# XCiT attention folded into a star-ReLU block: q's last rows in two transfers, three fixed v buffers, a k square on two engines, w_out's first piece ahead of v's second tile, v's first tile in 256, 128 and 128 tokens

## The chip, the cores and the metric

The kernel runs on one core of one Trainium2 chip. The metric is the device time of one execution in microseconds (us); lower is better. The engines are named as in the profile: PE (TensorE matmuls) with PEld (its weight loads), DVE (VectorE), ACT (ScalarE), POOL (GpSimd, which here only issues DMAs), and SP (SyncE, which issues DMAs too).

## The reference

There are B = 4 batches of N = 6080 tokens with C = 256 channels, and a block with Dff = 2048.

```python
def _attn_ref(q, k, v, tau) -> np.ndarray:
    qn = q / (np.linalg.norm(q, axis=1, keepdims=True) + 1e-06)
    kn = k / (np.linalg.norm(k, axis=1, keepdims=True) + 1e-06)
    s = kn.transpose(0, 2, 1) @ qn / tau
    s = s - s.max(-1, keepdims=True)
    a = np.exp(s)
    a /= a.sum(-1, keepdims=True) + 1e-09
    return (v @ a).astype(np.float32)

def _moe_ref(x, w_in, w_out, s, b) -> np.ndarray:
    h = x @ w_in
    r = np.maximum(h, 0.0)
    g = s * (r * r) + b
    return (g @ w_out).astype(np.float32)
```

The attention matrix is channels by channels (256 x 256) for each batch, and needs the norms of q's and k's columns over all 6080 tokens of the batch. The output is 24320 x 256 in float32.

## The kernel before

**What is computed in which order.** For each batch the kernel sums the Gram matrix of k and q (`Gram.mm`, tile `s_ps`) and the squared norms (`squares`, `add_norms`, tile `n_ps`) over chunks of 512 tokens. `finish_ops` turns them into the inverse norms (`inverse`: Ln, Exp, on ACT), scales the Gram matrix (`scale`, on DVE), takes the exponential (`exps`, tile `eT`), and multiplies it into w_in: `wa` = softmax matrix times w_in, 256 x 2048, so that v @ a @ w_in becomes v @ wa. Then come 48 groups of 512 tokens of v (`NG` = 48, the last one of 256). A group is 16 steps (`FT` = 16); a step is one call of `mm1`, which makes 128 rows of h from the transposed v tile `vT`. Two steps share one tile `h_ps`, of which there are two buffers. `relu` (ACT) takes it, `square` (DVE or ACT) makes `g`, and a second product with w_out follows for the group before (`seven_items`, seven half-size products instead of eight; `plain_mm2` for the first and last group).

**What sets the order.** Nothing is scheduled by a planner: each instruction is issued where the Python code calls it (`po` keeps program order), so each engine works through its queue in that order. `at_step(s, f)` files a piece of side work under a step, `early` files the folds of w_in (`fold_one`) under steps 1, 3, 5 and 8, and the loop over `s` at the end of the file calls them. The Gram work of the next batch is side work of this kind.

**The head.** Batch 0 has no earlier group to hide behind. Its k and q are 13 chunks, the last two of 224 tokens each (112 partitions by 2). I call the last four c9 to c12, as the code's `c_, c0, c1, c2`. All transfers of k, q, v and the weights are issued by POOL in one queue, q's last rows (`load_last`) just ahead of v's first tile, in two pieces of which each is one chunk. Each POOL transfer uses one of eight semaphores in turn, and so waits for the landing of the transfer eight places before it. Once q's last rows are there, the chain is: squares (L201), column sums on PE (L270), Ln and Exp on ACT (L300), two short DVE instructions (L286, L288), `exps` (L331), row sums and the first fold of w_in on PE (L371, L376, L381), `scaled` on ACT and DVE (L352, L354), and the first `mm1` (L823). Ahead of the row sums PE transposes v's first tile: `turn_v(0, range(3))`, into a bank of the pool `ps_o`, and inside `first_block` the fourth block of 128 tokens, `turn_v(0, range(3, 4))`. The first `mm1` of group 0 is made in two parts, 384 and 128 tokens.

**v after the first two tiles.** `load_v(g)` (L495, POOL) brings a tile of 512 tokens in float16, `crossbar_v(g)` (L521, SP) transposes it by DMA at step (g-2)*16+6 into one of three `vT` buffers. The pool of v tiles has four buffers, and `load_v(g)` is called at step (g-4)*16+2 (tiles 3 and 4 both at step 2).

**Lines that the text names:** L130 `load`, L159 `load_last`, L174 `mm`, L201 and L203 `squares` on DVE and ACT, L216 and L230 `fold` and `into_first`, L266 and L270 `add_norms`, L325 `scale`, L359 `fold_mm`, L506 and L508 the transposes of `turn_v` and their copy, L565 `load_w_in`, L582 w_out's pieces, L697 `cast_w_out`, L823 and L836 `mm1`, L846 `relu`, L859 `square`, L911 `plain_mm2`, L1007 `seven_items`.

Of the kernel before, what the change touches and what calls it, by code (L numbers as in the profile page):

```python
# [16 lines left out]
def kernel(  # L17
# [37 lines left out]
    def po(ins):  # L55

        tc.keep_in_program_order(ins)
        return ins
# [10 lines left out]
    f3_pool = pool("f3_pool", 13)  # L69
    sm_pool = pool("sm", 1)  # L70
    apool = pool("apool", 2)
    vpool = pool("vpool", 4)
    vtpool = pool("vtpool", 3)
    rpool = pool("rpool", 2)
    gpool = pool("gpool", 2)
# [19 lines left out]
    JC = 4  # L95
# [16 lines left out]
    class Gram:  # L112
# [35 lines left out]
        def load_last(self, i):  # L148

            c = len(self.chunks) - 2  # L150
            at, np_, _ = self.chunks[c]
            if i == 0:
                self.raw[c] = qk_pool.tile([P, 2, JC, C], FP16, tag="qk", name="qk")
                for h in range(2):
                    t = self.raw[c][:, :, ts(h, 2)]
                    self.tiles[c + h] = t[:, 1], t[:, 0]
            rows = (k, q)[i][self.b, at:].rearrange("(p j) c -> p j c", j=JC)
            for js in [slice(0, JC)] if i == 0 else [ts(h, 2) for h in range(2)]:
                po(nc.gpsimd.dma_start(out=self.raw[c][:np_, i, js], in_=rows[:, js]))  # L159

        def cast(self, c):
# [21 lines left out]
        def norm_ops(self, c):  # L183
# [4 lines left out]

            at_end = self.b == 0 and c >= len(self.chunks) - NLATE

            def squares(a, js):
                def f():
                    if "sq" not in st:
                        if at_end:
                            st["sq"] = late_pool.tile([P, 2, jc, C], FP16, tag=f"sq{c}", name="sq")
                        else:
                            st["sq"] = sq_pool.tile([P, 2, JC, C], FP16, tag="sq", name="sq")
                    src = (qc, kc)[a][:np_, js, :]
                    if (a == 0 or c == len(self.chunks) - 1 if at_end else
                            a == 0 and (self.b > 0 or c % 2 == 0)):  # L200
                        po(nc.vector.tensor_mul(st["sq"][:np_, a, js, :], src, src))  # L201
# [35 lines left out]
            if self.b == 0 and c >= len(self.chunks) - NLATE - 1:  # L237
                ops = [lambda i=i: unfolded(i) for i in range(2)]
                if c == len(self.chunks) - NLATE:
                    return [squares(1, slice(0, jc)), [squares(0, ts(h, 2)) for h in range(2)], *ops]  # L240
                return [squares(1, slice(0, jc)), squares(0, slice(0, jc)), *ops]
            ops = []
            for h in range(0, jc, 4):
# [30 lines left out]
        def finish_ops(self):  # L274
# [88 lines left out]
            def first_block(n):  # L363

                two = [self.bank("wa_ps", CH, C)[:, 0, :n], h_tile("wa_ps")[:, 0, :n]]
                second = self.bank("wa_ps", CH, C)[:, :, :n]
                r_ps = ps_gram.tile([P, CH, C], FP32, tag="s_ps", name="r_ps")[:, :, 0]
                for j in range(CH):
                    exps(j)
                    for ch in range(CH):  # L370
                        po(nc.tensor.matmul(r_ps[:, ch : ch + 1], st["e"][:, j, ts(ch, P)],  # L371
                                            parts16, start=(ch == 0 and j == 0),
                                            stop=(ch == CH - 1 and j == CH - 1),
                                            skip_group_check=True))
                    for m in range(CH):
                        po(nc.tensor.matmul(two[m], st["e"][:, j, ts(m, P)],  # L376
                                            w_in16[:, j, :n],
                                            start=(j == 0), stop=(j == CH - 1)))
                for m in range(CH):
                    for j in range(CH):  # L380
                        po(nc.tensor.matmul(second[:, m], st["e"][:, j, ts(m, P)],  # L381
                                            w_in16[:, j, ds(n, n)], start=(m == 0 and j == 0),
                                            stop=(j == CH - 1), skip_group_check=True))
                copy = turn_v(0, range(3, 4))
                del v_tiles[0]
                st["rs"] = sm_pool.tile([P, CH], FP32, tag="rs", name="rs")
                po(nc.vector.reciprocal(out=st["rs"], in_=r_ps))
                for f0 in range(0, n, P):
                    for m in range(CH):
                        scaled(f0, P, m, two[m][:, ds(f0, P)])  # L390
                copy()
                for m in range(CH):
                    scaled(n, n, m, second[:, m])

            def fold_one(f0, n, m):
                def f():
# [93 lines left out]
    def load_v(g, js=None):  # L490
        t0, nj = group(g)
        js = js or slice(0, nj)
        if g not in v_tiles:
            v_tiles[g] = vpool.tile([P, TG // P, C], FP16, tag="v16", name="v16")
        po(nc.gpsimd.dma_start(  # L495
            out=v_tiles[g][:, js, :],
            in_=v_flat[t0 : t0 + nj * P, :].rearrange("(p j) c -> p j c", j=nj)[:, js]))

    def turn_v(g, js):
# [3 lines left out]
        vT_ps = ps_o.tile([P, CH, TG], FP16, tag="o_ps", name="vT_ps")  # L503
        for j in js:
            for ch in range(CH):
                po(nc.tensor.transpose(vT_ps[:, ch, ts(j, P)], v16[:, j, ts(ch, P)], ident16))  # L506
        cols = ds(js[0] * P, len(js) * P)
        return lambda: po(nc.vector.tensor_copy(out=vT_tiles[g][:, :, cols],  # L508
                                                in_=vT_ps[:, :, cols]))

    def transpose_v(g):
        turn_v(g, range(group(g)[1]))()
# [51 lines left out]
        cs = slice(0, CH) if co is None else slice(co, co + 1)  # L564
        po(nc.gpsimd.dma_start(out=w_in16[:, cs, f0:f1], in_=w_in_rows[:, cs, f0:f1]))  # L565

    load_v(0, slice(0, 3))
    load_w_in(0, 2 * P)
    load_w_in(2 * P, NW)
    load_v(0, slice(3, 4))  # L570
    load_w_in(NW, NW + 2 * P)
    load_w_in(NW + 2 * P, 2 * NW)
    load_w_in(2 * NW, 3 * NW)
    load_w_in(3 * NW, Dff)
    w_out_rows = moe_w_out.rearrange("(fo p) d -> p fo d", p=P)
    load_v(1)

    NPIECE = FT // 4
    w_pieces = []
    for i in range(NPIECE):  # L580
        w32 = qk_pool.tile([P, 4, C], FP32, tag="qk", name="w32")
        po(nc.gpsimd.dma_start(out=w32, in_=w_out_rows[:, ts(i, 4), :]))  # L582
        w_pieces.append(w32)
    load_v(2)
    s_bc = consts.tile([P, 1], FP32)
    po(nc.gpsimd.dma_start(out=s_bc, in_=moe_s.to_broadcast((P, 1))))
# [39 lines left out]
    for a in (1, 0):  # L626
        g0.rows[a].append(sum_rows[a])
        g0.add_norms(a)
    ops[c0][0]()
    add_rows(1, c0)  # L630
    ops[c1][0]()
    ops[c2][0]()
# [15 lines left out]
    g0.rows[0].extend(half)  # L648
    g0.add_norms(0)
    add_rows(0, c1)  # L650
    ops[c2][1]()
    g0.mm(c2, 0)
    ops[c2][2]()
    g0.mm(c2, 1, [0])
# [156 lines left out]
    def mm1(g, m):  # L811
# [5 lines left out]
        if fh == 0:  # L817
            h_tiles[g, i] = h_tile("h_ps")
        if g == 0 and i == 0:
            for cols in (slice(0, 3 * P), slice(3 * P, TG))[: 2 * fh]:  # L820
                for f in range(2):
                    for ci in range(CH):
                        po(nc.tensor.matmul(h_tiles[g, i][:, f, cols], g0.wa[:, ci, ts(f, P)],  # L823
                                            vT[:, ci, cols], start=(ci == 0),
                                            stop=(ci == CH - 1), skip_group_check=True))
            return
        h_ps = h_tiles[g, i][:, fh, :]
        for b, p0, p1 in segments(g):
# [275 lines left out]
```

## Time and profile before

| what | value |
|---|---|
| median of 3 runs | 713.14 us (713.06, 713.14, 714.91) |
| the profiled execution | 713.05 us, of which the span of the profile is 711.3 us |
| granted TensorE clock over the span | 0.998 |
| busy over the span | PE 692.2 us (97%), DVE 634.2 us (89%), ACT 547.8 us (77%), POOL 112.9 us (16%) |
| bytes moved by DMA | 83.81 MB, mean 118 GB/s |

The profile is one execution; its times count from the start of its span. A line of the timeline gives start, length, engine, source line, operation, tiles, shapes and count, and in brackets how long the engine was idle before and what ended that. Instructions of one engine that overlap are merged, so a merged line's length is less than the sum of its instructions. A line of busy time by stretch gives, for each engine, the busy time and in brackets the instructions, then the granted clock of TensorE (1.00 is full), the DMA share and GB/s. "Issue" in the DMA list is the moment at which a transfer was handed over; it lands some us later.

### The profile page before, as it was taken

What the parts mean: (1) busy time and instruction counts of PE and PEld (TensorE: products, weight loads), DVE (VectorE), ACT (ScalarE), POOL (GpSimd) and SP (SyncE); (2) the same over time, 40 slices, a digit from 0 to 9 for tenths busy, and PEclk for the clock granted to TensorE, in tenths of its full rate; (3) what the DMA queues carried; (4) which work ended last, traced back from release to release, by engine and by line L of the source; (5) the groups of instructions that cost most, each with busy time, mean ns of one, the idle gap of its engine ahead of it and who ended that gap; (6) DMA issues with size and microseconds to landing.
All of it is one profiled execution on the core that took longest, in us unless ns stands there. A gap on an engine that the chain in (4) does not pass through costs nothing.

```text
span 711.3 us, 17552 instructions
## 1 busy us (share of the span) xinstructions
PE 692.2 (97%) x7437; PEld 503.2 (71%) x7437; DVE 634.2 (89%) x906; ACT 547.8 (77%) x597; POOL 112.9 (16%) x189
## 2 busy tenths in 40 slices
PE   3799999999999999999999999999999999999998
PEld 2566777776777777777677777777768777777777
DVE  3899999999988989998999899998998888888886
ACT  5789877787787777778877777777877777877775
POOL 3543123202102221111010222211000000000000
PEclk9999999999999999999999999999999999999999
DMA  9999999647655978465861878748323323321202
GB/s 240 205 254 163 182 133 183 123 91 119 132 115 109 137 137 159 93 93 108 149 128 51 148 148 145 121 75 106 95 61 75 98 67 76 99 59 47 82 31 75
DMA packets 87694, 83.81 MB, mean 118 GB/s; under 512 B 56320, under 2 KB 63280, under 8 KB 87360
## 3 DMA queue, kind: packets, MB, share of 16 engines
q0 software_dynamic: 26848, 43.74, 38.9%
q1 hardware_dynamic: 60336, 37.71, 23.2%
q8 instruction: 58, 0.95, 0.6%
q10 hardware_dynamic: 432, 1.25, 0.4%
q14 instruction: 20, 0.16, 0.1%
HBM read 78.91 MB, written 24.90 MB: 146 GB/s over the span
## 4 chain that ended last, share of the span: by engine, by line
PE 95%; DMA 4%; ACT 1%; DVE 0%; issue 0%
PE h_ps L836 46%; PE o_ps L1007 40%; PE s_ps L174 4%; DMA qk<-in_k_dram 2%; PE wa_ps L428 1%; DMA raw<-in_q_dram 1%; DMA v<-in_v_dram 1%; PE o_ps L911 1%; PE o_ps L883 0%; PE wa_ps L359 0%; ACT sq L203 0%; ACT qk L165 0%; DVE f L216 0%; PE vT_ps L506 0%; PE h_ps L823 0%
## 5 line engine op out<-in xcount | busy, mean ns | idle before, releaser
L846 ACT ACTIVATE r<-h_ps 128x1024 f16<-128x1024 f32 (+1 forms) x384 | 388.5, 1013 | 144.6 <-PE h_ps L836 141.4
L836 PE MATMUL h_ps<-vT,wa 128*128 128x512 f16 (+7 forms) x1628 | 450.8, 364 | 0.0
L1007 PEld LDWEIGHTS <-S 128*128 128x128 f16 x2944 | 198.1, 98 | 84.3
L1007 PEld LDWEIGHTS <-g 128*128 128x128 f16 x2208 | 155.0, 98 | 74.1
L859 DVE TENSOR_TENSOR g<-r 128x2048 f16<-128x2048 f16 (+2 forms) x150 | 174.8, 1165 | 10.0 <-ACT r L846 9.6
L1007 PE MATMUL o_ps<-T,S 128*128 128x128 f16 x2208 | 183.1, 219 | 0.0
L836 PEld LDWEIGHTS <-wa 128*128 128x128 f16 x1628 | 136.2, 98 | 18.2 <-ACT wa L352 0.2
L1007 PE MATMUL o_ps<-w_out,g 128*128 128x128 f16 x1472 | 134.2, 219 | 0.0
L857 ACT ACTIVATE g<-r 128x1024 f16<-128x1024 f16 (+1 forms) x97 | 100.3, 1034 | 0.2
L864 DVE SCALAR_TENSOR_TENSOR o_sb<-o_ps,s_out,u 128x256 f32<-128x256 f32 x138 | 66.5, 482 | 35.9 <-PE o_ps L1007 34.2
L174 PE MATMUL s_ps<-qk 128*128 128x256 f16 (+1 forms) x384 | 70.7, 286 | 15.7 <-ACT qk L165 11.0
L495 POOL DMA_DIRECT2D v<-in_v_dram x49 | 32.2, 660 | 243.0 <-DMA vT<-v 150.4
L232 POOL DMA_DIRECT2D f<-f x33 | 28.8, 874 | 242.9 <-DVE f L216 159.4
L864 DVE SCALAR_TENSOR_TENSOR u<-o_ps,s_out,rowconst 128x256 f32<-128x256 f32 x138 | 66.0, 478 | 0.0
L1007 PE MATMUL o_ps<-w_out,S 128*128 128x128 f16 x736 | 63.5, 219 | 0.0
L1007 PE MATMUL o_ps<-N,g 128*128 128x128 f16 x736 | 63.4, 219 | 0.0
L936 DVE TENSOR_TENSOR S<-S,g 128x2048 f16<-128x2048 f16 (+1 forms) x47 | 56.4, 1201 | 1.2
L203 ACT ACTIVATE sq<-qk 128x1024 f16<-128x1024 f16 (+2 forms) x53 | 54.5, 1041 | 2.8 <-DVE f L216 1.8
L934 DVE TENSOR_TENSOR S<-g 128x2048 f16<-128x2048 f16 (+1 forms) x47 | 56.1, 1193 | 0.0
L940 DVE TENSOR_TENSOR S<-g,S 128x2048 f16<-128x2048 f16 x46 | 56.0, 1218 | 0.0
L938 DVE TENSOR_TENSOR S<-g 128x2048 f16<-128x2048 f16 x46 | 56.0, 1217 | 0.0
L174 PEld LDWEIGHTS <-qk 128*128 128x128 f16 (+1 forms) x384 | 32.9, 103 | 20.7 <-ACT qk L165 11.0
(110 smaller groups left out, 333.6 us busy)
## 6 DMA issues: line engine op xcount, KB each, us to landing
out_dram<-o_sb SPq DMA_DIRECT2D x41, 512.0 KB, 3.4
v<-in_v_dram POOLq DMA_DIRECT2D x46, 256.0 KB, 4.9
qk<-in_k_dram POOLq DMA_DIRECT2D x38, 256.0 KB, 6.5
qk<-in_q_dram POOLq DMA_DIRECT2D x37, 256.0 KB, 7.4
f<-f POOLq DMA_DIRECT2D x30, 128.0 KB, 3.2
out_dram<-o_sb SPq DMA_DIRECT2D x12, 256.0 KB, 3.3
vT<-v SPq DMA_TRANSPOSE x182, 3.4
w<-in_moe_w_out_dram POOLq DMA_DIRECT2D x4, 512.0 KB, 8.4
```

Of the source, the lines that this page charges most:

```text
L174: po(nc.tensor.matmul(self.s_ps[:, ch, :], qc[:np_, j, ts(ch, P)], kc[:np_, j, :], start=(c == 0 and j == 0 and ch == 0), stop=(c == len(s ...
L203: po(nc.scalar.activation(out=st["sq"][:np_, a, js, :], in_=src, func=AF.Square))
L836: po(nc.tensor.matmul(dst, wa[:, ci, ts(m, P)], src, start=(ci == 0), stop=(ci == CH - 1), skip_group_check=True))
L846: po(nc.scalar.activation(out=r16[:, :, i % 2, :n], in_=h_tiles.pop((g, i))[:, :, :n], func=AF.Relu))
L857: po(nc.scalar.activation(out=dst, in_=src, func=AF.Square))
L859: po(nc.vector.tensor_mul(dst, src, src))
L864: po(nc.vector.scalar_tensor_tensor(out=dst, in0=src, scalar=s_out, op0=ALU.mult, in1=add, op1=ALU.add))
L934: po(nc.vector.tensor_add(T[1], A21, A22))
L936: po(nc.vector.tensor_sub(T[2], T[1], A11))
L938: po(nc.vector.tensor_sub(T[3], A11, A21))
L940: po(nc.vector.tensor_sub(T[4], A12, T[2]))
L1007: po(nc.tensor.matmul(st[name][:, j, :], a()[:, i, ts(j, P)], w[:, i, :], start=first, stop=last, skip_group_check=True))
```

## The change

It has five parts, all in the order and size of pieces; the arithmetic is the same.

1. q's last chunk c12 (224 tokens) comes in two transfers of 112 tokens instead of one, and its square is two DVE instructions of 112x256 instead of one of 112x512.
2. k's square of chunk c10 was one ACT instruction of 128x1024; it is now 128x512 on ACT and 128x512 on DVE.
3. v's first tile comes in 256, 128 and 128 tokens (was 384 and 128). Its first 256 tokens are transposed ahead of the row sums, the other two blocks of 128 later: one before the first `mm1`, one between its matmuls, both into a bank of `ps_gram`, with one copy for the two. The first `mm1` is made in halves of 256 tokens, and the folds of step 1 stand between the halves.
4. The v tiles have three buffers with fixed names instead of a pool of four, and `load_v(g)` moves from step (g-4)*16+2 to (g-3)*16+2 (tile 3 stays at step 2).
5. w_out's first piece (512 KB) is issued ahead of v's second tile (256 KB) instead of behind it.

On the engines this makes: PE the same matmuls and transposes, in another order and with other widths; DVE two instructions more; ACT as many as before, one of them half as wide; POOL two DMAs more, both ahead of w_in's third piece (and one v tile fewer at step 2); SP the same.

```diff
-    vpool = pool("vpool", 4)
+    vpool = pool("vpool", 1)
...
-            for js in [slice(0, JC)] if i == 0 else [ts(h, 2) for h in range(2)]:
+            for js in [slice(0, JC)] if i == 0 else [slice(0, 2), slice(2, 3), slice(3, 4)]:
                 po(nc.gpsimd.dma_start(out=self.raw[c][:np_, i, js], in_=rows[:, js]))
...
-            def squares(a, js):
+            def squares(a, js, on_vector=False):
...
-                    if (a == 0 or c == len(self.chunks) - 1 if at_end else
-                            a == 0 and (self.b > 0 or c % 2 == 0)):
+                    if on_vector or (a == 0 or c == len(self.chunks) - 1 if at_end else
+                                     a == 0 and (self.b > 0 or c % 2 == 0)):
...
                 if c == len(self.chunks) - NLATE:
-                    return [squares(1, slice(0, jc)), [squares(0, ts(h, 2)) for h in range(2)], *ops]
+                    return [[squares(a, ts(h, 2), h == 1) for h in range(2)] for a in (1, 0)] + ops
+                if c == len(self.chunks) - 1:
+                    return [squares(1, slice(0, jc)), [squares(0, ts(h, 1)) for h in range(2)], *ops]
...
-                copy = turn_v(0, range(3, 4))
-                del v_tiles[0]
+                rest_v = turn_v(0, range(2, 4), ps_gram)
+                rest_v[0]()
                 st["rs"] = sm_pool.tile([P, CH], FP32, tag="rs", name="rs")
                 po(nc.vector.reciprocal(out=st["rs"], in_=r_ps))
                 for f0 in range(0, n, P):
                     for m in range(CH):
                         scaled(f0, P, m, two[m][:, ds(f0, P)])
-                copy()
-                for m in range(CH):
-                    scaled(n, n, m, second[:, m])
+
+                def rest():
+                    for f in rest_v[1:]:
+                        f()
+                    del v_tiles[0]
+                    for m in range(CH):
+                        scaled(n, n, m, second[:, m])
+
+                self.rest = rest
...
-            v_tiles[g] = vpool.tile([P, TG // P, C], FP16, tag="v16", name="v16")
+            slot = g if g < 3 else (0, 2, 1)[g % 3]
+            v_tiles[g] = vpool.tile([P, TG // P, C], FP16, tag=f"v{slot}", name="v16")
...
-    load_v(0, slice(0, 3))
+    load_v(0, slice(0, 2))
     load_w_in(0, 2 * P)
     load_w_in(2 * P, NW)
-    load_v(0, slice(3, 4))
+    for j in (2, 3):
+        load_v(0, slice(j, j + 1))
...
-    load_v(1)
-
...
         w_pieces.append(w32)
+        if i == 0:
+            load_v(1)
     load_v(2)
...
-    turn_v(0, range(3))()
+    turn_v(0, range(2))()
     first_block()
...
-            at_step(max(g - 4, 0) * FT + 2, lambda g=g: load_v(g))
+            at_step((g - 3) * FT + 2, lambda g=g: load_v(g))
...
-            for cols in (slice(0, 3 * P), slice(3 * P, TG))[: 2 * fh]:
+            for half in range(2 * fh):
+                cols = ts(half, TG // 2)
                 for f in range(2):
                     for ci in range(CH):
                         po(nc.tensor.matmul(h_tiles[g, i][:, f, cols], g0.wa[:, ci, ts(f, P)],
                                             vT[:, ci, cols], start=(ci == 0),
                                             stop=(ci == CH - 1), skip_group_check=True))
+                    if half == 0 and f == 0:
+                        g0.rest()
+                if half == 0:
+                    for fold in early.pop(1):
+                        fold()
             return
```

More of the change, by code (lines that the diff above doesn't have):

```diff
@@ L497, in load_v, with turn_v @@
             in_=v_flat[t0 : t0 + nj * P, :].rearrange("(p j) c -> p j c", j=nj)[:, js]))
-    def turn_v(g, js):
+    def turn_v(g, js, into=ps_o):
         v16 = v_tiles[g]
@@ L502, in turn_v, with turn @@
             vT_tiles[g] = vtpool.tile([P, CH, TG], FP16, tag="vT", name="vT")
-        vT_ps = ps_o.tile([P, CH, TG], FP16, tag="o_ps", name="vT_ps")
-        for j in js:
+        vT_ps = into.tile([P, CH, TG], FP16, tag="o_ps" if into is ps_o else "s_ps", name="vT_ps")
+        def turn(j):
             for ch in range(CH):
@@ L507, in turn_v @@
         cols = ds(js[0] * P, len(js) * P)
-        return lambda: po(nc.vector.tensor_copy(out=vT_tiles[g][:, :, cols],
+        copy = lambda: po(nc.vector.tensor_copy(out=vT_tiles[g][:, :, cols],
                                                 in_=vT_ps[:, :, cols]))
+        if into is not ps_o:
+            return [lambda j=j: turn(j) for j in js] + [copy]
+        for j in js:
+            turn(j)
+        return copy
     def transpose_v(g):
@@ L628 @@
         g0.add_norms(a)
-    ops[c0][0]()
+    for f in ops[c0][0]:
+        f()
     add_rows(1, c0)
@@ L650 @@
     add_rows(0, c1)
-    ops[c2][1]()
+    for f in ops[c2][1]:
+        f()
     g0.mm(c2, 0)
```

## The prediction

> **What bounds the kernel now.** I read the page first, then busy time by stretch, then the timeline of the head, engine by engine, and last the waits of POOL.
>
> The page's totals and chain:
>
> ```profile
> span 711.3 us, 17552 instructions
> PE 692.2 (97%) x7437; PEld 503.2 (71%) x7437; DVE 634.2 (89%) x906; ACT 547.8 (77%) x597; POOL 112.9 (16%) x189
> PE 95%; DMA 4%; ACT 1%; DVE 0%; issue 0%
> ```
>
> PE carries 95% of the chain. Busy time by stretch (columns PE, PEld, DVE, ACT, POOL, granted clock, DMA share, GB/s) says where PE is not busy:
>
> ```profile
> 22.56:25.98 3.42, 1.35 (x10) 0.96 (x11) 3.18 (x7) 2.65 (x4) 1.41 (x3) 1.00 1.13 211
> 25.98:29.39 3.41, 3.41 (x15) 2.22 (x16) 3.20 (x7) 2.69 (x3) 1.85 (x3) 0.50 1.11 207
> 32.80:36.22 3.42, 2.87 (x37) 1.86 (x36) 2.26 (x8) 2.30 (x6) 2.41 (x5) 1.00 1.39 194
> 34.50:35.05 0.55, 0.00 (x1) 0.01 (x1) 0.52 (x4) 0.18 (x1) 0.00 (x0) 1.00 1.44 189
> 35.05:700.00 664.95, 664.95 (x7175) 481.79 (x7176) 606.33 (x846) 521.70 (x565) 97.32 (x158) 1.00 0.62 113
> ```
>
> From 35.05 us on PE has no idle time at all, at full clock. The end is therefore the moment at which PE's unbroken row begins, plus a fixed amount of matmul work, plus stalls that the change may add. All five parts must be judged by that. The idle time to be had just before is 0.55 us. The timeline (PE, then ACT, then DVE) shows what the row begins with:
>
> ```profile
> 33.65 0.25 PE L270 MATMUL n_ps<-ones,sq 112*128 112x1 f16 x4
> ...
> 35.05 0.51 PE L506 MATMUL vT_ps<-ident,v 128*128 128x128 f16 x6 [0.55 <-DMA v<-in_v_dram]
> 35.44 0.20 PE L371 MATMUL r_ps<-parts,eT 128*128 128x1 f16 x2
> ...
> 36.76 1.05 PE L823 MATMUL h_ps<-vT,wa 128*128 128x384 f16 x8
> 37.65 0.60 PE L359 MATMUL wa_ps<-w_in,eT 128*128 128x256 f16 x4
> 38.08 1.03 PE L836 MATMUL h_ps<-vT,wa 128*128 128x512 f16 x4
> ...
> 41.11 1.46 PE L836 MATMUL h_ps<-vT,wa 128*128 128x512 f16 x6
> ...
> 34.87 0.91 ACT L331 ACTIVATE eT<-sm_t,r 128x256 f16<-128x256 f32 x2 [0.44 <-DVE r L288]
> ...
> 37.85 1.02 ACT L846 ACTIVATE r<-h_ps 128x1024 f16<-128x1024 f32 x1 [0.52 <-PE h_ps L823]
> ...
> 32.60 0.99 DVE L201 TENSOR_TENSOR sq<-qk 112x512 f16<-112x512 f16 x2 [0.16 <-DMA qk<-in_q_dram]
> ...
> 40.89 0.75 DVE L354 TENSOR_SCALAR wa<-wa_ps,rs 128x512 f16<-128x512 f32 x1
> ```
>
> PE waits for v at 35.05, but the six transposes are over, at a start every 0.056 us, by 35.39, and the row sums behind them need the first half of eT, an ACT instruction of 0.51 us begun at 34.87: 35.38. Two waits end together there. An earlier v alone can gain next to nothing.
>
> **The change part by part**
>
> *q's last chunk in two transfers.* From issue and time to landing, the two last q chunks (112 KB each) land at 24.82+7.8 = 32.6 and 26.14+7.0 = 33.14, so 112 KB pass in 0.56 us. Halves write packets half as large. w_in's pieces and v's 64 KB have such packets: w_in lands at 29.85+6.3 = 36.15, v's 64 KB at 31.02+5.4 = 36.4, so 0.25 to 0.35 us for 64 KB and about 0.3 for 56 KB. The first half lands near 32.9, the second near 33.2, 0.06 later than now; bounds 0 and +0.2. The square of the second half is shorter: DVE takes 0.69 us for 1024 columns and 0.43 for 512, so about 0.30 for 256, and the first half is done while the second arrives. The square ends at 33.2+0.02+0.30 = 33.52 instead of 33.59. PE cannot use all of it: its Gram matmuls ahead of the four column sums (three from 33.29, one per 0.109) hold it until 33.61 against 33.65 now. Gain 0.04 us.
>
> On this part a rule speaks against the change. The row above prices a 64 KB transfer in a busy queue at about 0.3 us. The Trainium skill, "DMA: Bandwidth & Descriptors", Bandwidth, says that transfers under 64 KB are dominated by descriptors and lists 0.95 us for 64 KB; by that, an estimate, two halves would land some 0.8 us later than one, and the head with them. No row here shows such a price with eight transfers in flight.
>
> *k's square on two engines.* ACT's half (0.63 us by the 112x512 row) is done at 30.22; DVE's half (0.43) fits between 30.22 and 30.75, where DVE idles 0.53 us until k's last rows land. The column sums already start at 30.70, and ACT's next square waits for the same landing. Gain 0. If DVE were late by the whole 0.43, Ln of k's norms would follow; ACT has 0.16 us there, so at most 0.3 lost.
>
> *v's first tile in three pieces.* The first piece lands at 27.38+7.62 = 35.00 now, 1.86 us after q, though 192 KB at the pace of q is 0.96. Bounds for 128 KB: 33.8 by the pace, 35.1 if only the lateness counts; I take 34.7, as 64 KB less go first. Four transposes end 0.22 us later, before eT at 35.34. w_in's first pieces move up by 0.25 us, hidden likewise. Two of the six transposes leave the idle time and join PE's unbroken row: +2 x 0.056 = +0.11 us. What is in front of the first L823 is unchanged and waits for wa from ACT, so it starts at 36.72. Then 2 matmuls of 256 (0.22), 2 transposes (0.11), 2 (0.22), 4 folds (0.43), 4 (0.43): 38.13 against 38.08. Net of the 0.04: +0.05 us.
>
> The tile h_ps is now complete only at the end of that row. relu starts at about 38.33 instead of 37.85, and behind it on ACT the next relu at 39.35 instead of 39.15; PE's third tile needs the first relu at 39.35 and comes to it at 39.43, just covered. On DVE the square behind relu (now 38.90) moves to 39.38, and with it what is queued behind: two wa blocks, a square, and the 512-wide wa block, now 40.89 to 41.64, then about 41.38 to 42.13. PE asks for that block at its fifth matmul after 41.11, at 41.97 now and 42.02 then. Stall 0.15 us; bounds 0 (DVE overlaps more) and 0.45 (it is late by all of relu's delay). From DVE's wait for relu at 43.23 (idle 0.39 now) it has caught up.
>
> *Fixed v buffers.* In POOL's queue tile g now stands where g+1 stood and waits for the same crossbar transposes as that one did:
>
> ```profile
> POOL v L495 <- DMA vT<-v: 150.4, 13, 14.2
> ```
>
> These waits are POOL's own and hold the same k and q loads behind them. I compared each tile's transposes with the landing of the next tile, which is where it will land: tile 4 would land at 59.20+3.9 = 63.1 for transposes that begin at 64.0, tile 8 4.4 us ahead, the others more. PE takes tile 4 at 91.3, after its transposes end at 85.0: 6.3 us of cover. Cost 0. At step 2, 256 KB less pass (about 1.25 us of the queue), which helps k's loads that are followed by nothing late.
>
> *w_out's piece ahead of v's second tile.* w_out lands at 36.02+7.2 = 43.2 now and about 42.0 then; its cast at 43.84 waits for DVE's own square, so gain 0. v's second tile slips by one w_out piece, 1.5 us, from 41.7 to 43.2; its transposes stand at 45.9. Cover 2.7 us; were it gone, PE would stall by the excess.
>
> Sum: +0.05 (L836 begins at 38.13) and +0.15 (the stall at 42.0) make +0.2 us on the profiled execution's own 713.05, that is 713.25. The profiled run lies 0.09 below the median of the runs shown, so 713.3.
>
> **The rivals**
>
> *The head gains.* If relu's delay is swallowed and v's earliness counts, the 0.55 us idle plus the 0.3 us by which v and w_in come earlier is all there is: -0.85, 712.2. For it: PE's wait is named as v. Against: eT ends at the same instant.
>
> *One more stretch at half clock.* After 1.35 us busy in 3.42 (39%), the next 3.41 us were granted 0.50. In 32.80 to 36.22 PE is busy 2.87 (84%); the change takes at most 0.3 of it, 75%, and 2.14 of 3.41 (63%) at 19.15 was still followed by full clock. If it came all the same inside the unbroken row it would cost 3.41 x 0.5 = 1.7 us: 714.9, where one of the runs before lies. The Trainium skill, "TensorE: Matmul & The Clock Gate", Part 1, says that this window runs free of the kernel's start; then its place changes from run to run, before and after alike.
>
> *v comes late: slower.* With three buffers tile 4 waits for the transposes of tile 2 at 58.6. If it took the 13.4 us that the slowest v tile took to land instead of 3.9, its transposes would begin at 72.6, 8.6 late, and PE would wait 8.6-6.3 = 2.3 us: 715.4. It decides from a landing after 70.3. Against: the bytes in flight there are the same as before.
>
> *It does not do what it says*, for instance because the scheduler keeps the old order, is excluded by the instructions of the changed program: order and widths on each engine are as described. I give it no chance of its own.
>
> **How the numbers follow.** The forecast's own bounds are +0 (no stall, L836 a little earlier) and +0.9 (q's landing +0.2, k's square +0.2, stall 0.45), so 713.0 to 714.0: 0.64; the head gains 0.13; half clock in the median 0.11; v late 0.09; anything unnamed 0.03. The range takes in the forecast, the gaining head and the half-clock case: 712.2 to 714.9. 0.3% (2.1 us) is about what a measurement of this kernel can tell from no change; below 711.0 only an unnamed cause leads (0.02), above 715.3 v being late and part of the unnamed (0.10), within it the rest (0.88).
>
> **What would show it.** PE idle ahead of L506 shorter and no idle after; L371 at 35.3 to 35.5; relu's first start near 38.3 and DVE's first square near 39.4; a stall of PE near 42.0 of 0.1 to 0.3; no wait of PE for vT at 91. Wrong if PE shows idle time after 45, if L371 starts more than 0.4 us earlier, or if a second stretch of clock 0.50 stands in the span.

## The result, and the profile after

| what | before | after |
|---|---|---|
| median | 713.18 us (22 runs, 712.85 to 714.91) | 714.78 us (22 runs, 713.64 to 716.53) |
| the profiled execution, its span | 713.05 us, 711.3 us | 714.4 us, 712.7 us |

The ratio is 1.0018 with a 95% interval of 1.0013 to 1.0024: the change costs 0.9 to 1.7 us, and the medians lie 1.6 us apart. The forecast was 713.3 us.

The page after, the two lines that answer to those of before (the span; the shares of the chain that ended last by engine):

```profile
span 712.7 us, 17560 instructions
PE 93%; DMA 4%; DVE 1%; ACT 1%; issue 0%; POOL 0%; POOLq 0%; DVEq 0%
```

DVE has come into the chain with 1%, where it had 0%. Busy time by stretch (PE, PEld, DVE, ACT, POOL, granted clock, DMA share, GB/s) says where:

```profile
34.22:34.84 0.62, 0.00 (x2) 0.01 (x1) 0.58 (x4) 0.25 (x1) 0.54 (x1) 1.00 1.44 187
...
65.00:70.00 5.00, 4.09 (x41) 2.74 (x40) 4.93 (x6) 4.66 (x7) 2.57 (x5) 1.00 1.01 152
70.00:700.00 630.00, 630.00 (x6909) 458.95 (x6907) 573.26 (x787) 489.80 (x523) 83.55 (x134) 1.00 0.58 109
```

The same stretch of the kernel before:

```profile
65.00:70.00 5.00, 5.00 (x58) 3.77 (x57) 4.97 (x7) 5.00 (x9) 2.51 (x5) 1.00 1.04 207
```

PE is idle in the head, as before, and for 0.91 us between 65 and 70, where before it had no idle time. From 70 on it is busy without a gap in both. By the starts of the groups, the excess arises there and nowhere else: group 2 begins at 62.03 against 61.97, group 3 at 77.28 against 75.92, and the last matmul ends at 709.81 against 708.46. So up to group 2, where the forecast put its +0.2, the excess is 0.06 us in this profile, and 1.3 us come on top, in two gaps of PE:

```profile
65.01 0.44 PE L1032 MATMUL o_ps<-w_out,g 128*128 128x128 f16 x5
66.16 0.29 PE L1032 MATMUL o_ps<-w_out,g 128*128 128x128 f16 x2 [0.70 <-DVE g L884]
...
67.42 0.40 PE L1032 MATMUL o_ps<-T,S 128*128 128x128 f16 x4 [0.21 <-DVE S L959]
```

Both wait for DVE. Idle time counts from the end of the last matmul; from start to start of the matmuls the two gaps are 0.86 and 0.37 us longer than the usual 0.056 us, which is nearly all of the 1.3 us. The list of waits of after from 45 to 70 us (engine, line, what was waited for; total, times, longest) shows what DVE itself waited for:

```profile
DVE s_out L754 <- DMA s_bc<-in_moe_s_dram: 1.4, 1, 1.4
...
PEld L1032 <- DVE g L884: 0.9, 1, 0.9
PE o_ps L1032 <- DVE g L884: 0.7, 1, 0.7
```

`s_out` is one DVE instruction of 0.15 us at step 14, which multiplies the scalar s (0.5 KB, broadcast by one of POOL's transfers) by a constant. Neither the prediction nor the diff mentions it. DVE's timeline before:

```profile
48.65 1.22 DVE L668 TENSOR_TENSOR acc<-w,w 128x1024 f32<-128x1024 f32 x1
49.78 0.15 DVE L735 TENSOR_SCALAR s_out<-s_bc 128x1 f32<-128x1 f32 x1
```

and after:

```profile
48.70 1.22 DVE L687 TENSOR_TENSOR acc<-w,w 128x1024 f32<-128x1024 f32 x1
51.33 0.15 DVE L754 TENSOR_SCALAR s_out<-s_bc 128x1 f32<-128x1 f32 x1 [1.41 <-DMA s_bc<-in_moe_s_dram]
```

DVE comes to it at the same time in both. Before, s had landed at 48.91, 0.87 us ahead; after, it landed at 51.30. From there to 66 us DVE has no idle time of more than 0.12 us in either kernel, so that next to nothing is caught up: the square of g that PE needs begins at 64.89 instead of 63.40, 1.49 us late, and PE pays what its own slack does not cover. The square before and after:

```profile
63.40 1.22 DVE L859 TENSOR_TENSOR g<-r 128x2048 f16<-128x2048 f16 x1
```

```profile
64.89 1.22 DVE L884 TENSOR_TENSOR g<-r 128x2048 f16<-128x2048 f16 x1
```

The list of DMA issues from 30 to 52 us (KB, us from issue to landing) has the transfer before and after:

```profile
s_bc<-in_moe_s_dram POOLq DMA_DIRECT2D x1, 0.5 KB, 9.4
```

```profile
s_bc<-in_moe_s_dram POOLq DMA_DIRECT2D x1, 0.5 KB, 11.5
```

It is issued at 39.5 before and 39.8 after; nearly all of the lateness is gathered between issue and landing. Of the 2.39 us, 0.98 are those by which the transfer ahead of it, v's third tile, is late (49.72 instead of 48.73); the other 1.41 are s's own, which landed 1.59 us behind that tile instead of 0.18.

### The profile page after: what moved, and what is told of

Read it like the earlier page. It is cut to its first block, busy times and chain, and to the rows that moved or that the text cites. A ratio compares the mean times of both kernels' runs of the same rounds, so it can differ in the third digit from the quotient of the medians.

```text
span 712.7 us, 17560 instructions
## 1 busy us (share of the span) xinstructions
PE 690.9 (97%) x7437; PEld 502.3 (70%) x7437; DVE 634.5 (89%) x908; ACT 547.9 (77%) x597; POOL 114.3 (16%) x191
## 4 chain that ended last, share of the span: by engine, by line
PE 93%; DMA 4%; DVE 1%; ACT 1%; issue 0%; POOL 0%; POOLq 0%; DVEq 0%
PE h_ps L861 45%; PE o_ps L1032 40%; PE s_ps L174 4%; DMA qk<-in_q_dram 3%; PE wa_ps L436 1%; DMA v<-in_v_dram 1%; PE o_ps L908 0%; DVE g L884 0%; PE o_ps L936 0%; PE wa_ps L361 0%; ACT g L882 0%; ACT r L871 0%; POOL qk L143 0%; DVE o_sb L889 0%; DVE S L959 0%
## 5 line engine op out<-in xcount | busy, mean ns | idle before, releaser
L174 PE MATMUL s_ps<-qk 128*128 128x256 f16 (+1 forms) x384 | 68.8, 279 | 17.0 <-ACT qk L165 10.8
L203 ACT ACTIVATE sq<-qk 128x1024 f16<-128x1024 f16 (+3 forms) x53 | 54.1, 1033 | 3.2 <-DVE f L216 1.8
```

The costliest lines, as they stand in the source:

```text
L174: po(nc.tensor.matmul(self.s_ps[:, ch, :], qc[:np_, j, ts(ch, P)], kc[:np_, j, :], start=(c == 0 and j == 0 and ch == 0), stop=(c == len(s ...
L203: po(nc.scalar.activation(out=st["sq"][:np_, a, js, :], in_=src, func=AF.Square))
```

## The experiments

The theory (A): DVE's wait for s is the excess, and s is late because the change puts two small transfers more into POOL's queue. The rivals: that the wait is a symptom; that the order of w_out and v's second tile makes s late; that part 4, the fixed v buffers, costs something. Each group of four runs has its own runs of the kernel before beside it: 713.21, 713.25 and 713.26 us.

**Part 4 undone: the pool of four again** (u4_pool_of_four).

```diff
-    vpool = pool("vpool", 1)
+    vpool = pool("vpool", 4)
...
-            slot = g if g < 3 else (0, 2, 1)[g % 3]
-            v_tiles[g] = vpool.tile([P, TG // P, C], FP16, tag=f"v{slot}", name="v16")
+            v_tiles[g] = vpool.tile([P, TG // P, C], FP16, tag="v16", name="v16")
...
-            at_step((g - 3) * FT + 2, lambda g=g: load_v(g))
+            at_step(max(g - 4, 0) * FT + 2, lambda g=g: load_v(g))
```

Expected: 

> The changed kernel, with part 4 undone: a pool of four v tiles, tile g loaded at step (g-4)*16+2, tiles 3 and 4 both at step 2. Theory S: s stands ahead of tiles 3 and 4 in the queue, so its landing does not change and the ratio to the kernel before stays at 1.0012 to 1.0024. Rival V, the fixed buffers cost the time: the ratio falls to 1.0000 to 1.0006.

Measured: 721.65 us, ratio 1.012 (1.0104 to 1.0135). Every theory missed this: without part 4 the change costs not 1.6 but 8.4 us. PE is idle for 4.3 us at 62.45, where it waits for the transposed third tile of v (tile 2):

```profile
PE h_ps L860 <- DMA vT<-v: 4.3, 1, 4.3
```

The run of four fixed buffers below explains it.

**Part 5 undone: v's second tile ahead of w_out again** (u5_v1_first).

```diff
+    load_v(1)
     NPIECE = FT // 4
...
-        if i == 0:
-            load_v(1)
```

Expected: 

> The changed kernel, with part 5 undone: v's second tile is issued ahead of w_out's first piece again. Theory S: the same bytes go ahead of s, s lands as late as in the changed kernel (50.5 to 51.5 us), and the ratio to the kernel before stays at 1.0012 to 1.0024. Rival: if it is the order of these two that costs, it falls to 1.0000 to 1.0006.

Measured: 714.46 us, ratio 1.002 (1.0011 to 1.0029). The order of the two transfers is not the cause of most of it. The profiled execution does not show the other runs' reason, because in it a second stretch of half clock fell into the head (stretch, busy times, granted clock):

```profile
25.98:29.39 3.41, 3.41 (x15) 2.21 (x16) 3.19 (x7) 2.69 (x3) 1.62 (x3) 0.50 1.13 210
29.39:32.80 3.41, 3.41 (x30) 2.66 (x29) 2.62 (x7) 1.29 (x3) 2.47 (x4) 0.63 1.23 195
```

Its row sums begin at 36.51 instead of 35.16, so all of DVE's work is later and the wait for s is gone from it. This is the half-clock rival of the prediction, seen once, at a price of 1.1 to 1.35 us (against the run a_s_out_later, where q's last rows landed at the same 33.22 and the row sums begin at 35.40, it is 1.1); the changed kernel's own profile has no such stretch (1.00 and 1.00 there).

**DVE's multiplication by s ten steps later** (a_s_out_later).

```diff
-    at_step(14, lambda: po(nc.vector.tensor_scalar_mul(
+    at_step(24, lambda: po(nc.vector.tensor_scalar_mul(
```

Expected: 

> The changed kernel, with the one small DVE instruction that scales s (s_out) filed under step 24 instead of step 14. Theory S: in the profile after, DVE stands at this instruction from 49.92 to 51.33 us, because s itself lands only at 51.30; everything behind it on DVE is 1.4 us late, and PE pays 0.86 and 0.37 us at 65 and 67 us, where the products of group 1 need DVE's squares and sums. With the instruction moved, DVE does not wait, PE shows no idle time after 46 us, and the ratio to the kernel before falls from 1.0018 to between 0.9998 and 1.0006. Rival V: the three v buffers, with tile 4 loaded at step 18, disturb DVE or the transfers; then nothing changes and the ratio stays at 1.0013 to 1.0024. Rival L: the head is later by itself; then it stays too.

Measured: 713.45 us, ratio 1.0012 (1.0003 to 1.0021); the medians differ by 0.24. With nothing changed but the place of one instruction of 0.15 us, the median loses 1.33 of its 1.6 us. The ratio, though, lies between theory S (up to 1.0006) and the rivals (from 1.0013), and its interval reaches into both. The runs fall into two groups, six at 713.24 to 713.45 and five at 714.28 to 715.9, so that the median stands just inside the lower one. s still landed at 51.06 and PE had no idle time at 65 to 67.5. In the profiled execution (714.4) PE stood instead at 40.51 for 1.05 us:

```profile
PE wa_ps L361 <- DMA w_in<-in_moe_w_in_dram: 1.1, 1, 1.1
```

It waited for a piece of w_in, which one of the sixteen DMA engines brought at 41.52, 1.1 us behind the next slowest. That is the second place at which the same late queue can be paid for. The other runs of the upper group may be of this kind, which only this one profile shows.

**s and b ahead of w_out** (b_s_first).

```diff
+    s_bc = consts.tile([P, 1], FP32)
+    po(nc.gpsimd.dma_start(out=s_bc, in_=moe_s.to_broadcast((P, 1))))
+    b_bc = consts.tile([P, 1], FP32)
+    po(nc.gpsimd.dma_start(out=b_bc, in_=moe_b.to_broadcast((P, 1))))
     NPIECE = FT // 4
...
     load_v(2)
-    s_bc = consts.tile([P, 1], FP32)
-    po(nc.gpsimd.dma_start(out=s_bc, in_=moe_s.to_broadcast((P, 1))))
-    b_bc = consts.tile([P, 1], FP32)
-    po(nc.gpsimd.dma_start(out=b_bc, in_=moe_b.to_broadcast((P, 1))))
```

Expected: 

> The changed kernel, with the transfers of s and b issued ahead of w_out's first piece instead of behind v's third tile. Theory S: s lands before 43 us, DVE's wait at step 14 is gone, the ratio to the kernel before is 0.9998 to 1.0006, as with the instruction moved. Should these two small transfers hold up the DMA engines wherever they stand, as a gap of about 1 us in the landings at 49 to 51 us suggests, then w_out and v's second tile land up to 2 us later; v's second tile has 2.7 us of cover, so the ratio may be 1.0005 to 1.0015. Rivals V and L: 1.0013 to 1.0024 as before.

Measured: 713.58 us, ratio 1.0009 (1.0001 to 1.0018). s landed at 41.80 and the wait is gone. But two transfers of 0.5 KB now stand ahead of w_out's first piece, which landed at 44.69 instead of 43.13, and the list of waits has a new line there:

```profile
PE o_ps L936 <- DVE w_out L716: 0.5, 1, 0.5
```

PE waits for the piece that DVE casts. Here too five of the 11 runs are at 714.16 or above, and the profiled one (714.16) is of them. So a and b remove the same wait by two ways, and both bring back 1.2 to 1.3 us of the median, but in nearly half of their runs something else holds the time up. What the wait alone is worth is seen better in the next run.

**The wait alone, made in the kernel before** (d_before_s_late): s and b behind v's tiles 3 and 4.

```diff
-    po(nc.gpsimd.dma_start(out=s_bc, in_=moe_s.to_broadcast((P, 1))))
...
-    po(nc.gpsimd.dma_start(out=b_bc, in_=moe_b.to_broadcast((P, 1))))
...
+    at_step(2, lambda: po(nc.gpsimd.dma_start(out=s_bc, in_=moe_s.to_broadcast((P, 1)))))
+    at_step(2, lambda: po(nc.gpsimd.dma_start(out=b_bc, in_=moe_b.to_broadcast((P, 1)))))
```

Expected: 

> The kernel before, with one thing changed: the transfers of s and b are issued behind those of v's tiles 3 and 4 (step 2) instead of ahead of them, so that s lands near 51.3 instead of 48.9; it reproduces the wait without any of the five parts. Theory A (the wait of DVE for s is the whole excess): DVE waits 1.2 to 1.7 us for s at about 49.8, PE is idle by 0.7 to 1.2 us in all at 63 to 68, and the median is 714.0 to 714.6. Theory B (the wait is a symptom, and the excess of the changed kernel comes from its other stalls): DVE waits, but catches up before PE needs it; 713.1 to 713.4.

Measured: 714.95 us, ratio 1.0024 (1.0014 to 1.0033), a little above theory A's range. s landed at 51.59; the waits from 45 to 70 us:

```profile
DVE s_out L733 <- DMA s_bc<-in_moe_s_dram: 1.6, 1, 1.6
...
PE o_ps L1007 <- DVE g L859: 0.9, 1, 0.9
```

These are the same two lines as in the changed kernel, 0.2 us larger, in a kernel that has none of the five parts. The wait for s is enough by itself to make the whole excess.

**Part 4 alone on the kernel before** (f_before_three_fixed).

```diff
-    vpool = pool("vpool", 4)
+    vpool = pool("vpool", 1)
...
-            v_tiles[g] = vpool.tile([P, TG // P, C], FP16, tag="v16", name="v16")
+            slot = g if g < 3 else (0, 2, 1)[g % 3]
+            v_tiles[g] = vpool.tile([P, TG // P, C], FP16, tag=f"v{slot}", name="v16")
...
-            at_step(max(g - 4, 0) * FT + 2, lambda g=g: load_v(g))
+            at_step((g - 3) * FT + 2, lambda g=g: load_v(g))
```

Expected: 

> The kernel before with part 4 alone: three v buffers of fixed names, and tile g loaded at step (g-3)*16+2. Theory A (the part costs nothing, as POOL's waits hold the same loads behind them): 713.0 to 713.4, PE without idle time after 35, s at 48.9 as before, and POOL waiting for transposes before v's tile 4. Theory B (the part moves loads in the head and disturbs w_out or s): s or w_out later by 0.5 us or more, 713.7 to 714.5.

Measured: 713.2 us, ratio 1.0 (0.9991 to 1.0009): theory A. PE has no idle time after 35.1; POOL waits 9.3 us before v's tile 4. s landed at 49.49 instead of 48.91, though the queue ahead of it is the same as in the kernel before: by so much two profiles can differ of themselves.

**Two transfers fewer** (c_two_fewer), and each of them alone (u1_q_whole, u3_v_256_256). The first has both edits, the other two one each:

```diff
-            for js in [slice(0, JC)] if i == 0 else [slice(0, 2), slice(2, 3), slice(3, 4)]:
+            for js in [slice(0, JC)] if i == 0 else [ts(h, 2) for h in range(2)]:
...
-                    return [squares(1, slice(0, jc)), [squares(0, ts(h, 1)) for h in range(2)], *ops]
+                    return [squares(1, slice(0, jc)), [squares(0, slice(0, jc))], *ops]
```

```diff
-    for j in (2, 3):
-        load_v(0, slice(j, j + 1))
+    load_v(0, slice(2, 4))
```

Expected of both together: 

> The changed kernel with two transfers fewer in the head: q's last chunk in one transfer (and one square of 112x512), and v's first tile in 256 and 256 tokens; all else as changed. Theory A (the two extra small transfers make w_in, v's third tile and so s late): w_in's 512-column piece lands near 40.4 again instead of 41.7, s near 49 to 50 instead of 51.3, DVE waits for s by less than 0.3 us, PE has no idle time at 65 to 67.5, and the median comes to 713.3 to 713.6. Theory B (s is late for another reason, for instance w_out's piece ahead of v's second tile): s lands at 51 again, PE is idle for about 0.9 us at 65 to 67.5, 714.5 to 714.9. In both the head may be 0.1 to 0.3 us later, since q's second half is squared in one piece.

Expected of q's chunk whole: 

> The changed kernel with q's last chunk in one transfer again (one transfer fewer in the head) and its square in one instruction; v's first tile still in 256, 128 and 128 tokens. The run with both small transfers put back was at 713.3 with s at 50.35, just 0.12 us ahead of DVE. Theory A1 (each extra transfer holds back what is behind it by about half): s near 50.8, DVE waits 0.3 to 0.7 us, and since the earlier runs put about 0.4 us of slack between DVE's wait and PE's, PE is idle 0 to 0.3 us: 713.3 to 713.9. Theory A2 (the two 64 KB pieces of v are what counts, q's halves are nothing): as the changed kernel, 714.4 to 714.9.

Expected of v in 256 and 256: 

> The changed kernel with v's first tile in 256 and 256 tokens (one transfer fewer), q's last chunk still in two transfers. Theory A1 (each extra transfer counts alike): as the run with q's chunk whole, 713.3 to 713.9, s near 50.8. Theory A2 (v's 64 KB pieces are what counts): no wait of DVE for s and no idle time of PE at 65 to 67.5, 713.2 to 713.5.

| kernel | median, us | ratio (interval) | s landed | DVE waits for s | GB/s in 36 to 38, 38 to 40 us |
|---|---|---|---|---|---|
| before | 713.18 | | 48.91 | no | 196, 184 |
| v in 256 and 256 | 713.36 | 1.0005 (0.9997 to 1.0014) | 49.69 | no | 186, 191 |
| q whole | 713.43 | 1.0003 (0.9994 to 1.0012) | 49.95 | no | 176, 160 |
| both | 713.3 | 1.0 (0.9991 to 1.0009) | 50.35 | no | 183, 211 |
| changed kernel | 714.78 | 1.0018 (1.0013 to 1.0024) | 51.30 | 1.4 us | 156, 132 |

Theory A holds: without the two transfers the excess is gone. Taking out either one alone brings back nearly all of it. For v's pieces both readings allowed that time; for q's halves A2 expected the changed kernel's, so the reading that only v's pieces count falls. The landings do not follow the count of transfers as closely as A1 said (49.7 and 50.0 where 50.8 was expected, and 50.35 with both removed). What decides is whether s lands before DVE comes for it, at 49.8 to 50.4 in these four: a threshold, not a slope; with both removed it landed only 0.04 us ahead. s's own tail varies too: behind v's third tile it took 0.2 us in the kernel before and with q whole, 0.6 with v in 256 and 256, 1.2 with both and 1.6 in the changed kernel, where ten DMA engines had brought it by 49.0 and the last at 51.3. Why some engines are so late with it stays open; it was not tried further.

One landing does follow the transfers in all fourteen profiles. w_in's last piece (512 columns) landed at 41.55 to 42.90 in the seven kernels with two transfers more ahead of it, and at 40.40 to 41.01 in the seven with one or none. With s it is the same where its place in the queue was left alone: 50.49 to 51.84 in six, 48.91 to 50.35 in the other six.

**Two places in the queue, and nothing else** (h_before_two_tiny): the kernel before with two transfers of 0.5 KB into a tile that nothing reads.

```diff
     load_v(0, slice(3, 4))
+    pad = consts.tile([P, 2], FP32)
+    for i in range(2):
+        po(nc.gpsimd.dma_start(out=pad[:, i : i + 1], in_=moe_b.to_broadcast((P, 1))))
```

Expected: 

> The kernel before with two transfers of 0.5 KB more in POOL's queue, behind v's first tile and ahead of w_in's third piece; they bring b into a tile that nothing reads. No other byte, size or order changes. Theory A (what counts is the number of transfers, as POOL issues each only when the one eight places ahead has landed, so two small ones take two places of eight and fewer bytes are under way): w_in's 512-column piece lands near 41.5 instead of 40.4, s near 50 to 51 instead of 48.9, DVE waits 0.2 to 1.3 us, 713.3 to 714.6. Theory B (it is the smaller packets of the split transfers): w_in within 0.3 us of before, s by 49.4, no wait of DVE, 713.1 to 713.4.

Measured: 721.14 us, ratio 1.0116 (1.01 to 1.0132). Theory A in sign, and far outside its size. s landed at 51.74, where DVE waited only 0.14 us for it, as earlier waits had held DVE up too, and w_in's last piece (512 columns) at 42.78 instead of 40.40. Busy time by stretch of the kernel before (the last two columns are DMA share and GB/s):

```profile
36.00:38.00 2.00, 2.00 (x22) 1.51 (x19) 1.60 (x6) 1.14 (x4) 1.98 (x3) 1.00 1.29 196
38.00:40.00 2.00, 2.00 (x14) 1.15 (x12) 1.93 (x5) 1.72 (x2) 2.00 (x4) 1.00 1.17 184
```

of the changed kernel:

```profile
36.00:38.00 2.00, 2.00 (x20) 1.59 (x19) 1.68 (x5) 0.99 (x3) 2.00 (x4) 1.00 1.13 156
38.00:40.00 2.00, 2.00 (x14) 1.12 (x12) 1.36 (x4) 1.80 (x2) 2.00 (x4) 1.00 0.99 132
```

and of the kernel before with the two 0.5 KB transfers:

```profile
36.00:38.00 2.00, 2.00 (x19) 1.36 (x17) 1.59 (x6) 1.09 (x4) 2.00 (x4) 1.00 1.29 156
38.00:40.00 2.00, 2.00 (x14) 1.20 (x13) 1.87 (x5) 1.73 (x2) 2.00 (x4) 1.00 0.96 121
```

Two transfers that carry next to nothing lower the rate as the changed kernel's small pieces do. POOL issues a transfer only when the one eight places ahead has landed on the slowest of the sixteen DMA engines: here the fifth of w_in's six pieces came to stand eight places behind v's first piece, which landed on fifteen engines by 33.91 and on the last at 35.08, and POOL stood for 1.21 us and issued it at 35.37 (33.04 in the kernel before). A small transfer takes a place like a large one; that therefore fewer bytes are under way and the faster engines run dry is an inference from the rate. The size of the packets is not needed for it.

POOL's own time is a second part that no run separates from the places. Each issue takes it 0.5 to 0.8 us, and the two of 0.5 KB took it 1.17. In the runs a_s_out_later and b_s_first v's first piece was not late (33.8), and POOL issued w_in's last four pieces from 32.88 on without a wait; even so the last was issued at 34.98 instead of 33.72, and landed at 42.90 and 41.64.

Most of the 7.9 us is PE's waits from 40 to 70 us:

```profile
PE h_ps L839 <- DMA vT<-v: 4.9, 1, 4.9
...
PE o_ps L914 <- DVE w_out L700: 1.0, 1, 1.0
```

The second is the late queue again; the first, the larger, is the stall of the run with the pool of four. Behind it, from 68.7 to 72.1, the granted clock was 0.50, which by that clock is up to another 1.7 us.

**Four fixed buffers** (e_four_fixed), the changed kernel with one buffer more:

```diff
-            slot = g if g < 3 else (0, 2, 1)[g % 3]
+            slot = g % 4
```

Expected: 

> The changed kernel with four v buffers of fixed names instead of three (tile g in buffer g modulo 4), loads at the same steps. Theory C (in the pool of four of the earlier run it was a free buffer that did harm: POOL no longer stands before v's fifth tile until the transposes of the third have landed, so it issues k and q loads of the next batch some 8 us earlier, and these slow the transposes of tiles 2 and 3): POOL's wait of 11 us before v is gone, the transposes of tile 2 land after 64 instead of 60.1, PE waits for vT by 3 to 6 us near 62, and the time is 717 to 722. Theory D (it was the load of tile 4 at step 2, in the head, that did harm): the loads stand where the changed kernel has them, so no wait of PE for vT; 714.4 to 715.

Measured: 721.56 us, ratio 1.0114 (1.0098 to 1.0129): theory C. POOL's first load of a v tile after 50 us stands thus in its timeline in the kernel before, in the changed kernel, and with four fixed buffers:

```profile
59.20 0.53 POOL L495 DMA_DIRECT2D v<-in_v_dram  x1 [9.65 <-DVE w L689]
```

```profile
60.61 0.53 POOL L504 DMA_DIRECT2D v<-in_v_dram  x1 [11.14 <-DMA vT<-v]
```

```profile
51.12 0.53 POOL L504 DMA_DIRECT2D v<-in_v_dram  x1 [0.77 <-PE h_ps L861]
```

In the first two, POOL stands for 10 to 11 us until the four transposes of tile 2 have landed (58.64 and 60.05; POOL goes on 0.56 us later; the first line names DVE's work, which ended at about the same time). With a free buffer it goes straight on, and the next batch's k and q loads, which are queued behind, are issued at 52.75 to 54.91 instead of from 61.48 on. They run beside the transposes: the last of tile 2's took 13.5 us from issue to landing (54.57 to 68.08) instead of 5.6, and PE, which needs it at 62.8, is idle for 5.42 us. Behind that gap TensorE's granted clock was low (busy times by stretch, granted clock, DMA share, GB/s):

```profile
62.80:68.20 5.40, 0.00 (x0) 0.01 (x1) 5.22 (x7) 1.00 (x3) 0.00 (x0) 0.86 1.37 144
68.20:71.60 3.40, 3.38 (x11) 1.46 (x12) 0.94 (x1) 1.06 (x2) 0.00 (x0) 0.50 0.95 241
71.60:75.00 3.40, 3.40 (x27) 2.25 (x26) 0.00 (x0) 2.52 (x4) 1.06 (x2) 0.72 0.43 60
```

The half of 3.4 us and 0.28 of another 3.4 are some 2.6 us more. Together that is 8.0 us, against which stand the 1.3 us of the changed kernel's own two gaps, which this run does not have; its span is 7.4 us longer, and its head 0.5 us later. The wait for the buffer had kept that road clear. In the pool of four the kernel's text does not say which buffer a tile gets: the kernel before got one that waits, and the same code with two transfers added, or with the changed head, got one that is free.

The Trainium skill, "DMA: Bandwidth & Descriptors", Queues, rings and completion order, says that each DMA engine takes turns, packet by packet, between the queues that have work for it. That fits the 13.5 us beside the 5.6: transposes from SP's queue and loads from POOL's share the engines, and SP's go slower the more POOL has issued.

**The version to which the runs point** (i_two_fewer_s_later): the two transfers removed, and `s_out` at step 24.

Expected: 

> The version to which the runs point: the changed kernel without its two extra transfers, and with DVE's multiplication by s at step 24 instead of 14, so that neither late landing can hold DVE. Theory A (nothing of the other parts is worth anything): 713.1 to 713.3, as the kernel before. Theory B (w_out's piece ahead of v's second tile and the two blocks that follow later gain once the stall is gone): 712.5 to 713.0.

Measured: 713.34 us, ratio 1.0002 (0.9993 to 1.0011): theory A, 0.04 us above its range. The stall is gone and nothing is gained; no version here is faster than the kernel before.

## Why the prediction was right or wrong

The range held the median by 0.12 us, and "within 0.3%" was right, but the point missed by 1.5 us. That the range held is luck: the forecast's own bounds ended at 714.0, and the range went up to 714.9 only for a stretch at half clock, which the changed kernel's profile does not have. The sum's head was right to 0.13 us; a term was missing.

- **The head.** The timeline of after, PE, then ACT, then DVE:

```profile
35.16 0.20 PE L373 MATMUL r_ps<-parts,eT 128*128 128x1 f16 x2
...
38.00 1.03 PE L861 MATMUL h_ps<-vT,wa 128*128 128x512 f16 x4
...
38.20 1.94 ACT L871 ACTIVATE r<-h_ps 128x1024 f16<-128x1024 f32 x2 [1.15 <-PE h_ps L843]
...
39.26 0.69 DVE L884 TENSOR_TENSOR g<-r 128x1024 f16<-128x1024 f16 x1 [0.64 <-ACT r L871]
```

  The forecast was 38.13 for the first full `mm1` on unchanged q landings, 38.33 for relu and 39.38 for the square; all stand 0.12 to 0.13 earlier. The chunk ahead of q's last rows landed 0.22 earlier in this profile, and the row sums begin at 35.16, earlier than the 35.3 to 35.5 named; from there to the first full `mm1` PE needs 2.84 us, 0.2 more than before. The second half of the sum, the stall of PE near 42.0, came too: DVE's 512-wide wa block ended at 42.00, and the matmul that asks for it began 0.16 us late. The row of PE between 35 and 62 us came out 0.06 us later.
- **q's halves.** They landed 0.28 and 0.30 us after what was ahead of them, as the nearest rows said. The 0.95 us for a 64 KB transfer in the Trainium skill, "DMA: Bandwidth & Descriptors", Bandwidth, which by the prediction's estimate would have put the head 0.8 us back, is not seen for the piece itself. But its advice against small transfers was right in the end, by another way than its price: what was behind them paid.
- **The step that failed** is in that same part: "about 0.3 for 56 KB" was taken as the whole cost of a piece, and for v "w_in's first pieces move up by 0.25 us". What a transfer costs those behind it, in places of the queue and in POOL's time, was left out. w_out's first piece landed at 43.13 where "about 42.0" was forecast, v's second tile at 44.23 instead of 43.2, v's third tile at 49.72 instead of 48.73, and s at 51.30 instead of 48.91. The runs show the cost as a whole; s's own tail of 1.59 us, without which it would have landed at about 49.9, just as DVE came, has no explanation here.
- **"From DVE's wait for relu at 43.23 (idle 0.39 now) it has caught up"** was true of relu and stood for all that follows. DVE's next wait for a transfer, at step 14 with 0.87 us of slack, was not looked up. Its slack was in the profile of before: issued at 39.5, landing 9.4 us later, used at 49.78.
- **Part 4 at nothing** was right on the kernel before (713.2) and wrong as a part of this change: there it is worth 6.9 us, since without it POOL gets a free buffer for v's tile 5 and does not wait. "These waits are POOL's own and hold the same k and q loads behind them" names the mechanism; that these waits protect the transposes was not seen.
- **w_out ahead of v: gain 0, cover 2.7.** v's second tile was not late at PE. Undoing it gives 714.46 against 714.78; whether the 0.3 is real is not settled, as the two medians come from different groups of runs.
- **The rivals.** v late at 91 us did not happen: PE has no wait for v there. The gain of the head did not come. The half-clock stretch came in one profile of another kernel. The sign named for a wrong forecast, idle time of PE after 45, is the one that came.

## What to carry to other kernels

A transfer in a queue that waits for the landing some places ahead costs a place and the issuing engine's time as well as its own: before adding small transfers, list every small late thing behind them in that queue, with its landing and the moment at which it is used. On an engine with no idle time for 15 us, an early wait of 1.4 us for a scalar arrives at the end almost undiminished (1.3 us here), so place such an instruction where its operand has long landed. And before a wait for a buffer is removed, ask which transfers it holds back: here one buffer more cost 6.8 us (721.56 against 714.78).

## What the runs showed of the hardware that was not expected

- Two transfers of 0.5 KB in a queue of eight places lowered the DMA rate from 192 to 104 GB/s in the stretch 34 to 36 us and from 184 to 121 in 38 to 40, and held back w_in's last piece from 40.40 to 42.78 us.
- A transfer is as late as its slowest DMA engine: v's first piece had landed on fifteen engines at 33.56 and on the sixteenth at 34.79 in the changed kernel, and on all by 34.09 in the run with two transfers fewer.
- Crossbar transposes beside loads of another queue took 13.5 us from issue to landing where they took 5.6 with that queue held, and the gap of 5.42 us that this made on PE was followed by some 5.2 us at half clock.
